# A dynamic convolution with two gated layers on one core: another order of the sequence, a buffer per tap product, a split by bank

## The chip, the cores and the metric

The kernel runs on one core of a Trainium2 chip. The core has a matrix engine (PE, TensorE), a vector engine (DVE, VectorE), a scalar engine (ACT, ScalarE), a fourth engine for elementwise work (POOL, GpSimd), an engine that only issues transfers (SP, SyncE), and 16 DMA engines that carry the transfers of all queues. The metric is the device time of one execution in microseconds; less is better.

## The reference, cut to what matters

```python
def _attn_ref(x, weight_gen):                      # x 2 x 4096 x 192, 8 heads, 7 taps
    w = np.exp(weight_gen - weight_gen.max(-1, keepdims=True))
    w = w / (w.sum(-1, keepdims=True) + 1e-09)
    x_pad = np.concatenate([np.zeros((B, 6, D)), x], axis=1)
    x_unf = x_pad[:, np.arange(S)[:, None] + np.arange(7)[None, :], :].reshape(B, S, 7, 8, 24)
    return np.einsum('bshk,bskhg->bshg', w, x_unf)
...
x = x.reshape(8192, 192)
x = (1 / (1 + np.exp(-(x @ w_gate)))) * (x @ w_val) @ w_out      # 192 -> 1536 -> 192
h = x @ w_in;  out = (h * np.cos(h)) @ w_out2                    # 192 -> 2048 -> 192
```

Each token is a softmax-weighted sum of itself and the six tokens before it, per head. Then come two layers. x is float32; the five weight matrices arrive as 64-bit floats, 8 bytes a number.

## The kernel before, in words

**Layout.** The 8192 tokens lie on 128 partitions of 64 tokens each. A chunk is 4 tokens of every partition (512 tokens), 16 chunks in all. The six tokens of padding before a partition's first token belong to the partition before it, so chunk 0 needs one load of its own four tokens and, for the padding, two more loads from the neighbouring partitions (`load_x`); chunk 1 loads eight tokens and copies two from chunk 0's buffer on POOL. Later chunks load ten tokens in one transfer.

**The convolution of a chunk.** After the softmax of the chunk's weights (`softmax_ops`, DVE and one Exp on ACT), DVE makes seven products, one for each tap (`tap`). For chunks 0 to 2, PE transposes each product and adds the seven up in PSUM (`transposes`, two banks, one for each half of the partitions). Chunk 0 is made by `first_input`: its products go through two buffers (`product_tile`), so the third product waits until PE has read the first. Between the products PE runs matmuls on the identity, one after each of the first six and four after the last (`warm_up`). Chunks 1 and 2 have a buffer for each product (`conv_products`).

**High and low parts.** Every float32 operand of the layers is split into a high part that PE multiplies exactly and a low part, the rest. The transposed input of chunks 0 and 1 is split by `split_input` with `fast` set: first six instructions on ACT for high parts (`L349`), then four on DVE (`L351`), then ten subtractions on DVE for the low parts (`L355`).

**The layers.** A step of layer 1 takes 128 columns of gate and value weights: 18 matmuls of 512 columns (`hidden`, `L407`; the last six need the low parts of the input), a sigmoid on ACT (`gate`, `L509`), the product on DVE (`L512`), high part on ACT (`L547`), low part on POOL (`L548`), and two or more steps later 10 output matmuls (`L426`). The banks of a step are free again after its product, and there are two pairs of banks, so step 2's matmuls wait for step 0's gate and product. Twelve steps make a chunk of layer 1. The segments run layer 1 of chunks 0 and 1, then layer 2 and layer 1 in turn.

**The weights.** They stay on the chip, as units: units 0 and 1 of layer 1 serve one step each, units 2 to 6 two steps each; three output units (o0, o1, o2) serve four steps each. A unit has a gate half and a value half (192 KB each for units 0 and 1, 384 KB each for the others); an output unit has 768 KB. x for a later chunk is 960 KB. A unit is decoded from 64-bit floats by two ACT instructions (`L109`, `L112`) and one on DVE (`L114`), then ACT makes its high part (`L119`) and POOL its low part (`L121`, for output units `L183`). `decoding` is a chain over all units in the order of their use; one `next` finishes a unit and starts the ACT part of the next one. `late` holds the high and low parts until they are run.

**The order** is that of the program on each engine; an engine takes its instructions one after another, and what is written first on ACT, DVE or POOL also runs first. Loads are issued on SP's queue, and at the start also on ACT's queue (`act`). The program has eight semaphores for transfers, used in turn, so an issue can wait for an earlier transfer to land, and the instructions behind it on its engine wait as well.

## Time and profile before

| | us |
|---|---|
| median of three runs (lowest, highest) | 1270.26 (1268.09, 1271.26) |
| profiled execution | 1270.46 |
| its span | 1268.6 |
| PE busy in the span | 1230.6 |
| DVE, ACT, POOL busy | 902.2, 795.2, 710.8 |

An engine is busy while an instruction of its own runs; the time in brackets ahead of an instruction is how long its engine stood idle before it, and behind the arrow stands what ended that. The granted clock of PE is given as a share of 2.4 GHz: 1.00 is 2.4 GHz, 0.50 is 1.2 GHz.

### The profile page before, as it was taken

To read this page: it belongs to the slowest core of one execution; us is meant where nothing else is said; L and a number is where in the kernel's file an instruction comes from. 1 tells how busy PE (TensorE), PEld (TensorE's weight loads), DVE (VectorE), ACT (ScalarE), POOL (GpSimd) and SP (SyncE) were. 2 spreads that over 40 slices of the span, in tenths; PEclk is the share of its full clock that TensorE was granted. 3 is DMA by queue.
4 is the path that set the end of the run, shared out by engine and by line. 5 is a ranking of instruction groups with operands and counts; after the bars stand their busy time and mean duration, and the time that the engine had idled before them with its cause. 6 is when DMAs were issued, how large, how long until landed. Compare 5 with 4: busy or idle time off the path is not lost.

```text
span 1268.6 us, 26949 instructions
## 1 busy us (share of the span) xinstructions
PE 1230.6 (97%) x11076; PEld 1051.6 (83%) x11076; DVE 902.2 (71%) x1307; ACT 795.2 (63%) x1328; POOL 710.8 (56%) x529
## 2 busy tenths in 40 slices
...
GB/s 211 200 110 26 58 37 81 26 45 32 33 58 26 74 32 45 26 38 57 27 59 48 43 28 26 69 27 49 51 21 50 26 71 26 13 51 14 1 26 25
DMA packets 26971, 62.33 MB, mean 49 GB/s; under 512 B 2530, under 2 KB 7010, under 8 KB 26848
## 3 DMA queue, kind: packets, MB, share of 16 engines
...
## 4 chain that ended last, share of the span: by engine, by line
PE 71%; DVE 7%; ACT 5%; issue 2%; POOL 0%; DVEq 0%; ACTq 0%
PE ph L407 39%; PE po L426 31%; DVE acc L302 2%; DVE wk L512 1%; ACT L533 1%; ACT wk L509 1%; ACT wk L533 1%; ACT gh L547 1%; DVE wk L537 1%; DVE wk L520 1%; DVE va L436 1%; ACT wk L527 1%; PE pt L328 1%; DVE wk L528 1%; DVE wk L523 0%
## 5 line engine op out<-in xcount | busy, mean ns | idle before, releaser
L548 POOL TENSOR_TENSOR gl<-wk,gh 128x512 fp32r<-128x512 f32 x446 | 606.5, 1366 | 506.3 <-ACT gh L547 389.3
L407 PE MATMUL ph<-xT,unit 64*128 64x512 f32 x5760 | 776.6, 391 | 15.1 <-ACT unit L119 3.7
L407 PEld LDWEIGHTS ph<-xT,unit 64*128 64x128 f32 x5760 | 615.6, 186 | 113.9 <-DVE wk L512 10.5
L426 PE MATMUL po<-gh,outu 64*128 64x512 f32 x2688 | 557.2, 390 | 4.7 <-ACT gh L547 1.8
L426 PE MATMUL po<-gl,outu 64*128 64x512 f32 x1792 | 469.4, 387 | 4.5 <-POOL gl L548 4.4
L426 PEld LDWEIGHTS po<-gh,outu 64*128 64x128 f32 x2688 | 407.8, 184 | 52.3 <-DVE va L436 9.2
L547 ACT ACTIVATE gh<-wk 128x512 fp32r<-128x512 f32 (+1 forms) x450 | 282.8, 628 | 254.0 <-DVE wk L512 190.7
L426 PEld LDWEIGHTS po<-gl,outu 64*128 64x128 f32 x1792 | 321.2, 184 | 32.0 <-POOL gl L548 6.1
L512 DVE TENSOR_TENSOR wk<-ph,wk 128x512 f32<-128x512 f32 x192 | 131.9, 687 | 153.5 <-ACT wk L509 127.3
L537 DVE SCALAR_TENSOR_TENSOR wk<-ph,wk 128x512 f32<-128x512 f32 (+1 forms) x258 | 167.0, 686 | 39.6 <-ACT wk L533 39.6
L533 ACT ACTIVATE wk<-wk,sin_bias 128x512 f32<-128x512 f32 (+1 forms) x258 | 171.2, 713 | 9.9 <-DVE wk L523 3.3
L509 ACT ACTIVATE wk<-ph 128x512 f32<-128x512 f32 x192 | 114.0, 594 | 63.7 <-PE ph L407 62.9
L520 DVE TENSOR_SCALAR wk<-ph 128x512 f32<-128x512 f32 x129 | 88.0, 683 | 71.3 <-PE ph L407 64.5
L527 ACT ACTIVATE wk<-ph 128x512 int32<-128x512 f32 x129 | 75.7, 587 | 78.5 <-PE ph L407 77.8
L276 DVE TENSOR_TENSOR pr<-xp,sm 128x768 f32<-128x768 f32 x89 | 101.0, 1137 | 2.2 <-PE pt L328 1.2
L302 DVE TENSOR_TENSOR acc<-acc,pr 128x768 f32<-128x768 f32 x78 | 100.9, 1294 | 0.4
L523 DVE SCALAR_TENSOR_TENSOR wk<-wk,ph 128x512 f32<-128x512 f32 x129 | 88.2, 684 | 4.4
L528 DVE TENSOR_TENSOR wk<-wk,ph 128x512 f32<-128x512 int32 x129 | 87.4, 678 | 0.0
L436 DVE TENSOR_TENSOR va<-po,va 128x512 f32<-128x512 f32 x32 | 22.0, 688 | 38.4 <-PE po L426 32.2
L355 DVE TENSOR_TENSOR xT<-pt,xT 64x256 fp32r<-64x256 f32 (+1 forms) x76 | 27.3, 414 | 21.5 <-ACT xT L349 21.3
L121 POOL TENSOR_TENSOR unit<-wf,unit 128x768 fp32r<-128x768 f32 (+1 forms) x11 | 22.9, 2080 | 31.6 <-ACT unit L119 31.6
L349 ACT ACTIVATE xT<-pt 64x256 fp32r<-64x256 f32 (+1 forms) x68 | 20.5, 377 | 23.4 <-PE pt L328 23.3
...
## 6 DMA issues: line engine op xcount, KB each, us to landing
...
rawo<-in_moe_w_out_dram SPq DMA_DIRECT2D x7, 768.0 KB, 20.2
...
```

The lines of the kernel that those rows point to most:

```text
L276: nc.vector.tensor_tensor(out=out.rearrange("p t (h g) -> p t h g", g=G), in0=xp[c][:, k:k + TC, :].rearrange("p t (h g) -> p t h g", g=G) ...
L302: nc.vector.tensor_tensor(out=acc, in0=acc, in1=last, op=ALU.add)
L407: nc.tensor.matmul(ps[i], lhsT=u.t[r, w, (s + i) % NQ, c0:c0 + P], rhs=xt[r, x, s, :], start=n == 0, stop=n == len(terms) - 1,)
L426: nc.tensor.matmul(po[2 * i + a], lhsT=w[r, d0:d0 + P], rhs=g[r], start=first and g is gh and d0 < D, stop=last and g is gl,)
L509: nc.scalar.activation(out=self.w[0], in_=self.ps[0], func=AF.Sigmoid)
L512: nc.vector.tensor_tensor(out=self.w[0], in0=self.ps[1], in1=self.w[0], op=ALU.mult)
L520: nc.vector.tensor_scalar(out=w, in0=u, scalar1=0.25, scalar2=ROUND_MAGIC, op0=ALU.add, op1=ALU.add)
L528: nc.vector.tensor_tensor(out=w, in0=w.bitcast(I32), in1=u, op=ALU.subtract)
L533: nc.scalar.activation(out=w, in_=w, func=AF.Sin, scale=-SIN_SCALE, bias=sin_bias)
L537: nc.vector.scalar_tensor_tensor(out=w, in0=self.ps[i][:, r], scalar=TWO_PI, in1=w, op0=ALU.mult, op1=ALU.mult)
L547: nc.scalar.activation(out=gh, in_=w, func=AF.Copy)
L548: eng.tensor_tensor(out=gl, in0=w, in1=gh.bitcast(F32), op=ALU.subtract)
```

## The change

It has four parts. (1) The chunks start at each partition's eighth tile and wrap round (`ROT` = 8), so chunk 0 has its padding in the same partition and comes in one transfer of ten tokens; chunk 1 loads four tokens and copies six from chunk 0's buffer; the chunks that need padding from the neighbouring partition are now the last two, 14 and 15. The weights of the softmax of chunk 0 and of chunks 1 and 2 come in two transfers in place of one. (2) `first_input` uses `conv_products`, with a buffer for each product, and the ten matmuls on the identity between them are gone. (3) The high parts of the split of chunks 0 and 1 go by bank: those of the first bank on ACT, those of the second on DVE, five instructions each. (4) The value halves of units 3 to 6 are issued on SP's queue and not on ACT's, and `first_input` takes three steps of `decoding` where it took two.

```diff
--- before.py
+++ after.py
@@ -59,6 +59,7 @@
     DA = P
     DC = D - DA
     NQ = D // HP
+    ROT = PAD + TC - PAD % TC
     LAG = 4
 
     xf = x.rearrange("b s d -> (b s) d")
@@ -211,13 +212,17 @@
     group_at = {t0 // TC: g for g, (t0, _) in enumerate(groups)}
     sm = {}
 
-    def load_group(g, tiles, tag, q=nc.sync):
-        t0, t1 = groups[g][0], groups[g + tiles - 1][1]
-        pool = opool if tag == "o" else fpool
+    def load_group(g, tag, q=nc.sync):
+        t0, t1 = groups[g]
+        pool = fpool if tag == "wf" else opool
         s = pool.tile([P, (t1 - t0) * H, K], F32, name="sm", tag=tag)
-        q.dma_start(
-            out=s.rearrange("p a k -> p (a k)"), in_=wgr[:, t0:t1, :].rearrange("p t c -> p (t c)")
-        )
+        cuts = sorted({t0, t1, min(max(t0, T - ROT), t1)})
+        for a, b in zip(cuts, cuts[1:]):
+            r = (a + ROT) % T
+            q.dma_start(
+                out=s[:, (a - t0) * H:(b - t0) * H, :].rearrange("p a k -> p (a k)"),
+                in_=wgr[:, r:r + b - a, :].rearrange("p t c -> p (t c)"),
+            )
         for t in range(t0, t1):
             sm[t] = (s, t0)
 
@@ -248,12 +253,14 @@
 
     xp = {}
 
-    def load_x(c, queues=(nc.sync, nc.sync)):
-        t0 = c * TC
+    def load_x(c):
+
+
+        t0 = (c * TC + ROT) % T
         pool, tag = (xpool, "xp") if c else (tpool, "xC")
         t = pool.tile([P, TC + PAD, D], F32, name="xp", tag=tag)
-        h = max(0, PAD - t0)
-        if c == 0:
+        h = PAD if c == 1 else max(0, PAD - t0)
+        if h and c != 1:
             for b in range(B):
                 nc.gpsimd.memset(t[b * per_batch:b * per_batch + 1, 0:h, :], 0.0)
         nc.sync.dma_start(out=t[:, h:, :], in_=xr[:, t0 - PAD + h:t0 + TC, :])
@@ -262,7 +269,7 @@
         elif h:
             for b in range(B):
                 p0 = b * per_batch
-                queues[b % 2].dma_start(
+                nc.sync.dma_start(
                     out=t[p0 + 1:p0 + per_batch, 0:h, :], in_=xr[p0:p0 + per_batch - 1, T - h:T, :]
                 )
         xp[c] = t
@@ -304,7 +311,7 @@
 
     def conv_products(c):
 
-        big = tpool.tile([P, K - 3, TC, D], F32, name="prs", tag="xA" if c % 2 == 0 else "xB")
+        big = tpool.tile([P, K - 3, TC, D], F32, name="prs", tag="xA" if c == LEAD else "xB")
         att[c] = [big[:, k] for k in range(K - 3)] + [product_tile(), product_tile(), acc_tile()]
         for k, pr in enumerate(att[c]):
             tap(c, k, pr)
@@ -343,8 +350,9 @@
             v = p[h][src, i * TC * HP:(i + 1) * TC * HP].rearrange("p (t n) -> p t n", n=HP)
             yield xt[dst, x, s].rearrange("p (t h n) -> p h t n", h=2, n=HP)[:, h], v
 
-    def high(eng, xt, p, slot):
-        for hi, v in columns(xt, 0, p, slot):
+    def high(xt, p, slot, engines):
+
+        for (hi, v), eng in zip(columns(xt, 0, p, slot), engines):
             if eng is nc.scalar:
                 eng.activation(out=hi, in_=v, func=AF.Copy)
             else:
@@ -371,13 +379,11 @@
     def split_input(xt, p, fast):
 
 
-        for slot in (OWN[0], OTHER[0], OWN[1]) if fast else OWN:
-            high(nc.scalar, xt, p, slot)
-        yield
-        if fast:
-            for slot in OTHER[1:]:
-                high(nc.vector, xt, p, slot)
-        for slot in (OWN[0], *OTHER[:2], OWN[1], OTHER[2]) if fast else OWN:
+        slots = (OWN[0], *OTHER[:2], OWN[1], OTHER[2]) if fast else OWN
+        for slot in slots:
+            high(xt, p, slot, (nc.scalar, nc.vector if fast else nc.scalar))
+        yield
+        for slot in slots:
             low(xt, p, slot)
         if not fast:
             exchange(xt)
@@ -385,15 +391,15 @@
     def first_input():
 
         p = [ps_o.tile([P, N], F32, name="pt", tag=f"po{2 * h}") for h in range(2)]
-        for k in range(K):
-            pr = product_tile()
-            tap(0, k, pr)
-            transposes(p, pr, k == 0, k == K - 1)
+        for k, _ in enumerate(conv_products(0)):
+            transposes(p, att[0][k], k == 0, k == K - 1)
             yield
         xt = xT[1, 0] = tpool.tile([P, 2, NQ, N], F32R, name="xT", tag="xA")
-        for _ in split_input(xt, p, True):
+        ops = split_input(xt, p, True)
+        next(ops)
+        yield
+        for _ in ops:
             pass
-        yield
 
     def hidden(u, c0, xt):
 
@@ -469,7 +475,7 @@
         nc.scalar.activation(out=o.rearrange("p t (x d) -> p t x d", d=HP)[:, :, 0::2, :], in_=p0, func=AF.Copy)
         nc.vector.tensor_copy(out=o[:, :, HP:DA], in_=p1[:, :, 0, :])
         nc.vector.tensor_tensor(out=o[:, :, DA:D], in0=p1[:, :, 1, :], in1=o[:, :, DA:D], op=ALU.add)
-        nc.sync.dma_start(out=outr[:, c * TC:(c + 1) * TC, :], in_=o)
+        nc.sync.dma_start(out=outr[:, (c * TC + ROT) % T:(c * TC + ROT) % T + TC, :], in_=o)
 
 
     xT = {}
@@ -631,8 +637,9 @@
     with tc.manual_schedule():
         nc.gpsimd.memset(sin_bias, SIN_BIAS)
         make_identity(nc, ident)
-        load_group(0, 2, "o", nc.scalar)
-        load_x(0, (nc.sync, nc.scalar))
+        load_group(0, "va", nc.scalar)
+        load_x(0)
+        load_group(1, "o", nc.scalar)
         sp, act = nc.sync, nc.scalar
         units1[0].load(sp, 0)
         units1[0].load(act, 1)
@@ -689,27 +696,27 @@
         for ops in [s0] * 3 + [s1] * 2 + [s0] * 2 + [s1] * 3:
             next(ops)
         nc.scalar.activation(out=warm, in_=sin_bias, func=AF.Sigmoid)
+        units1[3].load(sp, 1)
         load_x(1)
         units1[4].load(sp, 0)
+        units1[4].load(sp, 1)
         outs1[1].load(sp)
-        units1[5].load(sp, 0)
         for _ in s0:
             pass
         warm_up(NWARM)
         for k, _ in enumerate(first_input()):
-            if k in (3, 5):
+            if k in (5, 6):
+                next(decoding)
+            if k == 5:
+                run(late)
+            if k == K:
+                run(late)
                 next(decoding)
                 run(late)
-            if k == 2:
-                units1[3].load(act, 1)
-                units1[4].load(act, 1)
-            if k == K:
-                units1[5].load(act, 1)
-                units1[6].load(sp, 0)
-                units1[6].load(act, 1)
-                outs1[2].load(sp)
-            else:
-                warm_up(1 if k < K - 1 else 4)
+        for i in 5, 6:
+            units1[i].load(sp, 0)
+            units1[i].load(sp, 1)
+        outs1[2].load(sp)
         for st in steps[:2]:
             st.mm_high()
 
@@ -795,9 +802,9 @@
             if layer == 1 and j == st.nj - 2 and c + 2 < NCH:
                 load_x(c + 2)
                 if c + 4 in group_at and group_at[c + 4] > 2:
-                    load_group(group_at[c + 4], 1, "wf")
+                    load_group(group_at[c + 4], "wf")
             if layer == 2 and c == 0 and j == 5:
-                load_group(2, 1, "wf")
+                load_group(2, "wf")
         for q in waiting:
             q.mm_out()
         steps[-1].finish()
```

**What the change moves, on ACT.** Before, from the decoding of unit 2 (`wf<-raw 128x768`) to the first gate (`wk<-ph`) and the high part of unit 2 (`unit<-wf 128x768`); the two rows `DMA raw<-in_moe_w_val_dram` issue the value halves of units 5 and 6, `wf<-rawo` decodes o0, and a name like DMAHW4 is one of the eight semaphores of transfers:

```order
L109 ACTIVATE wf<-raw 128x768 [waits DMAHW1_49]
L112 ACTIVATE raw<-raw 128x768
L119 ACTIVATE unit<-wf 128x384 [waits DVE_49]
L349 ACTIVATE xT<-pt 128x4x64 [waits PE_49] x2
L349 ACTIVATE xT<-pt 64x4x64 x4
L136 DMA raw<-in_moe_w_val_dram 64x3x512 [waits DMAHW4_49]
L136 DMA raw<-in_moe_w_val_dram 64x3x512 [waits DMAHW6_49]
L109 ACTIVATE wf<-rawo 128x768 [waits DMAHW2_49,Pool_49]
L112 ACTIVATE rawo<-rawo 128x768
L509 ACTIVATE wk<-ph 128x512 [waits PE_49]
L119 ACTIVATE unit<-wf 128x768 [waits DVE_49,Activation_49]
```

The same place now, up to the high part of o0 (`outu<-wf`); the first `wf<-raw 128x768` is unit 2, the second, after o0, is unit 3:

```order
L110 ACTIVATE wf<-raw 128x768 [waits DMAHW7_49,DMAHW0_49]
L113 ACTIVATE raw<-raw 128x768
L357 ACTIVATE xT<-pt 128x4x64 [waits PE_49]
L357 ACTIVATE xT<-pt 64x4x64 x4
L120 ACTIVATE unit<-wf 128x384 [waits DVE_49]
L110 ACTIVATE wf<-rawo 128x768 [waits DMAHW1_49,Pool_49]
L113 ACTIVATE rawo<-rawo 128x768
L120 ACTIVATE unit<-wf 128x768 [waits DVE_49]
L110 ACTIVATE wf<-raw 128x768 [waits DMAHW3_49,DMAHW2_49,Pool_49]
L113 ACTIVATE raw<-raw 128x768
L515 ACTIVATE wk<-ph 128x512 [waits PE_49]
L120 ACTIVATE outu<-wf 128x4x192 [waits DVE_49]
```

The issues are gone from between the split of chunk 0 (`xT<-pt`) and the decoding of o0; the decoding of unit 3 now stands ahead of the first gate, and waits for two transfers.

**On DVE.** Before, the seven taps of chunk 0 (`pr<-xp,sm`), the decoding of units 0 and 1 between them, the four high parts (`CAST`) and the first low parts (`xT<-pt,xT`):

```order
L276 TENSOR_TENSOR pr<-xp,sm 128x768 [waits DMAHW2_49,DMAHW3_49,DVE_49,Pool_49]
L276 TENSOR_TENSOR pr<-xp,sm 128x768
L276 TENSOR_TENSOR pr<-xp,sm 128x768 [waits DVE_49,PE_49]
L276 TENSOR_TENSOR pr<-xp,sm 128x768 [waits DMAHW1_49,DVE_49,PE_49]
L114 SCALAR_TENSOR_TENSOR wf<-wf,raw 128x384 [waits DMAHW5_49,DMAHW4_49,Activation_49]
L276 TENSOR_TENSOR pr<-xp,sm 128x768 [waits DVE_49,PE_49] x2
L114 SCALAR_TENSOR_TENSOR wf<-wf,raw 128x384 [waits DMAHW6_49,DMAHW0_49,Activation_49]
L276 TENSOR_TENSOR pr<-xp,sm 128x768 [waits DVE_49,PE_49]
L351 CAST xT<-pt 64x4x64 [waits PE_49,Activation_49] x2
L351 CAST xT<-pt 64x4x64 x2
L355 TENSOR_TENSOR xT<-pt,xT 128x4x64 x2
L355 TENSOR_TENSOR xT<-pt,xT 64x4x64 x2
```

The same place now, the seven taps into `prs`, `pr` and `acc`:

```order
L283 TENSOR_TENSOR prs<-xp,sm 128x768 [waits DMAHW1_49,DVE_49]
L283 TENSOR_TENSOR prs<-xp,sm 128x768 x3
L283 TENSOR_TENSOR pr<-xp,sm 128x768 x2
L115 SCALAR_TENSOR_TENSOR wf<-wf,raw 128x384 [waits DMAHW4_49,DMAHW3_49,Activation_49]
L283 TENSOR_TENSOR acc<-xp,sm 128x768
L115 SCALAR_TENSOR_TENSOR wf<-wf,raw 128x384 [waits DMAHW6_49,DMAHW5_49,Activation_49]
L359 CAST xT<-pt 128x4x64 [waits PE_49]
L359 CAST xT<-pt 64x4x64 x4
L115 SCALAR_TENSOR_TENSOR wf<-wf,raw 128x768 [waits DMAHW7_49,DMAHW0_49,Activation_49]
L363 TENSOR_TENSOR xT<-pt,xT 128x4x64 [waits Activation_49]
```

The taps no longer wait for PE, the high parts wait for PE alone and not for ACT, and the decoding of unit 2 stands between the high and the low parts.

**On SP.** Before, the first issues (`xp` is x, `rawo` an output unit):

```order
L259 DMA xp<-in_x_dram 128x768
L265 DMA xp<-in_x_dram 63x1152
L136 DMA raw<-in_moe_w_gate_dram 64x3x256 x2
L136 DMA raw<-in_moe_w_gate_dram 64x3x512
L168 DMA rawo<-in_moe_w_out_dram 128x4x384
L136 DMA raw<-in_moe_w_gate_dram 64x3x512
L259 DMA xp<-in_x_dram 128x1536
L136 DMA raw<-in_moe_w_gate_dram 64x3x512
L168 DMA rawo<-in_moe_w_out_dram 128x4x384
```

And now:

```order
L266 DMA xp<-in_x_dram 128x1920
L137 DMA raw<-in_moe_w_gate_dram 64x3x256 x2
L137 DMA raw<-in_moe_w_gate_dram 64x3x512
L169 DMA rawo<-in_moe_w_out_dram 128x4x384
L137 DMA raw<-in_moe_w_gate_dram 64x3x512
L137 DMA raw<-in_moe_w_val_dram 64x3x512
L266 DMA xp<-in_x_dram 128x768
L137 DMA raw<-in_moe_w_gate_dram 64x3x512
L137 DMA raw<-in_moe_w_val_dram 64x3x512
L169 DMA rawo<-in_moe_w_out_dram 128x4x384
```

The two loads of x at the start became one of ten tokens, and each gate half from unit 3 on is followed by its value half; x of chunk 1 is half as wide and stands behind unit 3's value half.

## Rows read from the trace of the kernel before

**Rows 1.** Busy time of each engine (and instructions) by stretches of 80 us.
```profile
80.00:160.00 80.00, 70.36 (x630) 58.21 (x629) 56.84 (x67) 55.12 (x88) 53.99 (x37) 0.94 0.12 33
160.00:240.00 80.00, 79.69 (x714) 67.00 (x712) 63.56 (x95) 51.59 (x87) 47.29 (x35) 1.00 0.17 47
```
**Rows 2.** The same by stretches of 10 us: clock, DMA share and GB/s last.
```profile
0.00:10.00 10.00, 3.78 (x16) 3.48 (x16) 3.13 (x10) 3.08 (x5) 2.79 (x9) 1.00 0.83 193
10.00:20.00 10.00, 8.57 (x90) 7.03 (x90) 6.95 (x8) 4.75 (x9) 2.07 (x2) 1.00 1.11 189
20.00:30.00 10.00, 9.14 (x73) 6.72 (x72) 6.33 (x15) 2.47 (x7) 1.32 (x2) 1.00 1.06 255
30.00:40.00 10.00, 5.13 (x24) 3.14 (x25) 5.45 (x10) 7.46 (x11) 4.57 (x3) 0.72 1.10 184
```
**Rows 3.** Timeline of PE: start us, us, instructions, idle time before and its releaser.
```profile
22.10 1.11 PE L328 MATMUL pt<-ident,pr 64*128 64x64 f32 x16
...
35.41 1.65 PE L407 MATMUL ph<-xT,unit 64*128 64x512 f32 x6 [3.68 <-ACT unit L119]
...
42.89 2.22 PE L407 MATMUL ph<-xT,unit 64*128 64x512 f32 x18
...
61.81 5.21 PE L407 MATMUL ph<-xT,unit 64*128 64x512 f32 x30 [2.06 <-POOL unit L121]
...
72.12 2.04 PE L328 MATMUL pt<-ident,prs 64*128 64x64 f32 x62 [0.52 <-DVE wk L512]
...
82.64 2.65 PE L407 MATMUL ph<-xT,unit 64*128 64x512 f32 x18 [1.44 <-DVE xT L355]
```
**Rows 4.** Timeline of ACT; ACTq rows are issues of transfers.
```profile
16.06 0.55 ACT L109 ACTIVATE wf<-raw 128x384 f32<-128x384 f32 x1 [5.19 <-DMA raw<-in_moe_w_gate_dram]
...
23.25 2.00 ACT L349 ACTIVATE xT<-pt 128x256 fp32r<-128x256 f32 x6 [2.04 <-PE pt L328]
29.84 2.54 ACTq L136 DMA_DIRECT2D raw<-in_moe_w_val_dram  x2
32.49 0.89 ACT L109 ACTIVATE wf<-rawo 128x768 f32<-128x768 f32 x1 [7.24 <-DMA raw<-in_moe_w_gate_dram]
...
34.04 0.58 ACT L509 ACTIVATE wk<-ph 128x512 f32<-128x512 f32 x1
34.52 0.84 ACT L119 ACTIVATE unit<-wf 128x768 fp32r<-128x768 f32 x1
```
**Rows 5.** Timeline of DVE.
```profile
8.68 0.39 DVE L246 TENSOR_TENSOR sm<-sm,st 128x224 f32<-128x224 f32 x1
10.12 2.11 DVE L276 TENSOR_TENSOR pr<-xp,sm 128x768 f32<-128x768 f32 x2 [1.06 <-DMA xp<-in_x_dram]
...
17.08 0.56 DVE L114 SCALAR_TENSOR_TENSOR wf<-wf,raw 128x384 uint32<-128x384 uint32 x1 [1.77 <-ACT raw L112]
...
25.01 1.55 DVE L351 CAST xT<-pt 64x256 fp32r<-64x256 f32 x4 [3.49 <-ACT xT L349]
26.59 3.89 DVE L355 TENSOR_TENSOR xT<-pt,xT 128x256 fp32r<-128x256 f32 x10
...
111.03 7.03 DVE L276 TENSOR_TENSOR prs<-xp,sm 128x768 f32<-128x768 f32 x1
```
**Rows 6.** The transfer issued at 11.96 us: KB, us to landing.
```profile
xp<-in_x_dram SPq DMA_DIRECT2D x1, 768.0 KB, 17.9
```
**Rows 7.** The transfer issued at 15.88 us.
```profile
rawo<-in_moe_w_out_dram SPq DMA_DIRECT2D x1, 768.0 KB, 21.3
```
**Rows 8.** Timeline of POOL.
```profile
1.29 2.15 POOL L258 MEMSET xp<- 1x1152 f32 x2
10.05 0.50 POOL L261 COPY xp<-xp 128x384 f32<-128x384 f32 x1 [6.61 <-DMA xp<-in_x_dram]
...
37.87 1.29 POOL L548 TENSOR_TENSOR gl<-wk,gh 128x512 fp32r<-128x512 f32 x1
39.12 2.69 POOL L183 TENSOR_TENSOR outu<-wf,outu 128x256 fp32r<-128x256 f32 x2
```
## The prediction, made before the changed kernel was run

> **What bounds the kernel now.** I read the busy time by long stretches first. From 160 us on PE is busy 79.69 of 80 us at the full granted clock [rows 1]; its instructions are the same after the change, but for ten matmuls on the identity, so nothing can be won or lost there unless a new wait arises. Between 80 and 160 us PE is idle for 9.6 us, and the clock is granted at 0.94. The rest of what can move lies in the first 80 us. There the stretches of 10 us show the DMA engines busy throughout, at 193, 189, 255 and 184 GB/s [rows 2]: 1.93 MB have come by 10 us, 3.82 MB by 20, 6.37 MB by 30, 8.21 MB by 40. PE is busy only 5.13 us of the ten from 30 to 40 us, at a mean clock of 0.72.
>
> PE's timeline tells why [rows 3]. The transposes of chunk 0 end at 23.2 us (22.10 + 1.11). Step 2 starts at 35.41 us, after 3.68 us of idle time, and step 3 only at 42.89. At 61.81 us PE has waited 2.06 us for POOL's low part of a unit, and at 82.64 us 1.44 us for the low parts of chunk 1's input. On ACT [rows 4] the cause of 35.41 stands: the high parts of the input end at 25.25, and then ACT runs nothing until 32.49, an idle time of 7.24 us, because two issues of value halves stand in its queue and wait until 29.84 us and later for transfers to land. Behind them stand the decoding of o0, the first gate (34.04) and the high part of unit 2 (34.52). DVE's timeline [rows 5] shows the earlier part: the softmax ends at 9.07, the first tap starts at 10.12 when x has landed, and four high parts wait 3.49 us for ACT's.
>
> **The change, step by step.** All times are of the profiled execution (1270.46 us, a span of 1268.6 and 1.9 around it), which lies 0.2 us over the median of the runs.
>
> *Taps.* The weights of chunk 0's softmax (112 KB in place of 336) run beside one x transfer of 960 KB on the other queue; both were there by 10.12 before, with the same bytes. The first tap can start between 8.0 (my estimate for a softmax that ends 1 us before the 9.07 of now) and 10.1 (as now). I take 9.4, since the weights are fewer but share with a larger x. Seven taps without waits for PE cost at most 1.05 us each (two took 2.11 beside POOL's copy [rows 5]; the copy grows from 0.50 us to some 1.5 [rows 8], so I keep this price for all): 7.4. The decoding of unit 0 between them costs 0.56, the last 16 transposes 1.11. The transposes end at 18.5, 4.7 us earlier than 23.2. Transposes of 1.11 us a tap keep up with taps of 1.05 but for a few tenths.
>
> *High and low parts.* ACT made six in 2.00 us, DVE four in 1.55 [rows 4, 5]: five each, side by side, end at 20.5. On DVE the decoding of unit 2 now stands ahead of the low parts, twice the columns of one that took 0.56, so about 1.0; the low parts take 3.89 as before. They end at 25.4, against 30.48: 5.1 us earlier. The first high part on ACT also stands behind the decoding of unit 2; it costs nothing if that unit lands by 17, and up to 3 us if by 20.
>
> *The gate of step 0.* Here the change adds a wait. ACT is now free of issues, but ahead of the gate stand the decoding of o0 and of unit 3 (a pair of instructions takes 1.55 us, from 32.49 to 34.04) and the high part of unit 2; and behind the gate stands everything on ACT, so DVE's product and PE's step 2 wait too. When do the units land? Up to o0 the new order issues x 0.98 MB, softmax weights 0.34, units 0 and 1 0.79, unit 2 0.79 and o0 0.79: 3.69 MB, which by the rates of [rows 2] have come at 19.3; with unit 3 4.48 MB, at 22.6. A transfer lands later than its bytes in order: x of chunk 1, 5.27 MB with all issued before it, would be there at 25.7, and landed at 11.96 + 17.9 = 29.9 [rows 6], 4.2 us late; the output unit issued at 15.88, at 6.85 MB, would be there at 32.6 and landed at 37.2 [rows 7], 4.6 late. The lag is bounded by 0 and 4.6; I take 4.2. So o0 lands at 23.5, unit 3 at 26.8. ACT: o0 from 23.5 to 25.05, unit 2's high part to 25.9, a wait to 26.8, unit 3 to 28.35, then the gate. The first two steps' low terms are done by about 27 and are covered. From gate to step 2 it is 1.37 us (34.04 to 35.41): step 2 at 29.7, 5.7 us earlier; with a lag of 0, bound by the low parts, 8 us.
>
> *Step 3* comes after the output matmuls of step 0, and these need o0's low part and step 0's low part on POOL. o0's high part follows the gate on ACT, to 29.7; POOL then takes 2.69 for o0 and 1.29 for the step [rows 8], to 33.7; ten matmuls take about 1 us. Step 3 at 34.7, against 42.89: 8.2 us earlier. This is more than at step 2, because before, step 2 ran at the lower clock: six matmuls in 1.65 us, 0.275 each, where 18 take 2.22, 0.123 each [rows 3].
>
> *To the end of chunk 0.* The decoding of o1 stands ahead of step 2's gate. Its bytes, 6.45 MB, are there at 30.4, with the lag at 34.9; the gate comes at 36.5, then unit 4's high part, its low part on POOL and step 2's low part behind that, so the output matmuls of step 2 wait. This takes back 1.4 us: 6.8 remain. Later units arrive ahead of their use. One more step of decoding is done ahead of step 0, so each unit's low part stands one place further up in POOL's queue than before; the wait of 2.06 us at 61.81 should go, and with it the slow matmuls behind it (30 in 5.21 us, where 0.123 each give 3.7): 3.6 us. If POOL is as late as before, nothing. I take 3.6: 10.4.
>
> *Chunk 1.* The two-sided split takes 1.9 + 3.9 us where it took 7.2, so the wait of 1.44 us at 82.64 goes: 11.8. The other losses up to 160 us I leave as they are; they come from collisions of POOL and DVE, such as one tap of 7.03 us [rows 5], that no order shows, and I bound this by 4 us either way.
>
> *What costs nothing.* Chunks 14 and 15 get two memsets on POOL each (2.15 us for the larger pair [rows 8]) and two more transfers each; POOL is busy for only 47.29 of 80 us once the layers run evenly [rows 1] and x is loaded a whole layer-2 segment ahead. Without that cover it would be 2 to 4 us. SP's four more issues wait in place of ACT's; behind them stands x of chunk 1, which landed at 29.9 before, and whose products PE transposes at 72.1 [rows 3]. The load of x for chunk 1 is smaller by 0.39 MB, which is in the sums.
>
> Sum: 4.7 at the transposes becomes 5.7 at step 2, 8.2 at step 3, 6.8 at step 5, 10.4 at the end of chunk 0 and 11.8 after the split of chunk 1. 1270.46 - 11.8 = 1258.7, against the median 1258.5.
>
> **The clock.** The first transposes run at 69 ns each (16 in 1.11 us), those of chunk 1 at 33 (62 in 2.04) [rows 3], so PE was at the pace of the lower clock then, although the column of the granted clock reads 1.00 in those rows [rows 2]. Ten matmuls on the identity leave this stretch, and PE waits for the high parts without them. The Trainium skill, "TensorE: Matmul & The Clock Gate", section on the HAM clock gate, says that the throttled clock is the default, that only sustained activity releases it and that idle time takes it back; by it steps 0 to 2 would run at 1.2 GHz, and the time would be that of the first rival below, not the sum above. No row here shows the start without those matmuls.
>
> **Rivals.**
> - *Lower clock to step 3.* Step 2 (18 matmuls) and the ten output matmuls behind it take 0.15 us more each, 4.3, of which POOL's low parts cover 1.6; step 3 adds 2.7 before the clock is back. It gives back 2.7 to 5.4: 1261 to 1264. For it: the idle time at the start. Against it: steps 0 and 1 give PE 36 matmuls between 19 and 27 us.
> - *Weights set the pace.* The lag grows by 3 us, since all halves now go through one queue, and POOL's wait at unit 5 comes back because its work is as dense as before. 6.8 - 3 + 1.4 = 5: 1265. For it: the DMA engines are busy throughout.
> - *More is won.* Chunk 1 is relieved by the step of decoding that was done ahead; 4 us of its losses go: 1254.
> - *The gain is lost again.* POOL and DVE collide once more with a tap like the one of 7.03 us and a slow clock behind it, 5 + 3.4 us, in chunk 0 or 1: 1267, no change.
> - *Slower.* The gate of step 0 stands behind unit 3. If unit 3 landed after 32.5 (32.5 + 1.55 = 34.04), the gate would be later than now; at 38 us it costs 5.5, and 1276 is the time. Against it: by 38 us the rates bring 7.8 MB, and unit 3 needs 4.48.
>
> **Chances.** The forecast (1255 to 1262) 0.45, weights 0.20, clock 0.12, more 0.08, lost again or nothing done 0.10, slower 0.05. A difference of 0.3% (3.8 us) is about what a measurement of this kernel tells from none. Faster 0.85, same 0.10, slower 0.05. The range goes from 1252 (the forecast with the lag at 1 us and part of chunk 1's losses gone) to 1266 (weights at their worst); the cases outside hold about 0.18.
>
> **What would show it.** Right: the last transpose of chunk 0 ends near 18.5; no idle time of 7 us on ACT; step 2 near 29.7 and step 3 near 34.7; no waits of 2 us for a unit's low part near 50 us; the transposes of chunk 1 some 10 us earlier than 72.1. Wrong: ACT waiting for unit 3 or o1 past 30 and 38 us, PE at half clock through step 3, or a wait in chunks 14 and 15.

## The result

The changed kernel took 1255.09 us (median of 4 runs, 1254.03 to 1256.62), the kernel before 1269.17 beside it (1268.06 to 1271.26): a ratio of 0.9876, 95% interval 0.9858 to 0.9894. The forecast was 1258.5, its range 1252 to 1266. The profiled execution of after took 1254.05 us with a span of 1252.3, which is 16.3 us less than the span of before. One of the four executions of run 1 below took 1355.79 us at a mean clock of 0.85, a slow state that is not the kernel's, and is left out of that run's median.

Busy time by stretches of 10 us, and then of 80 us, of the changed kernel. The columns, here and in [rows 1, 2], are the stretch and its length, the busy time of PE, of PE's loading of weights, of DVE, ACT and POOL (with the number of instructions), the granted clock, the DMA share and GB/s:

```profile
0.00:10.00 10.00, 3.79 (x16) 3.49 (x16) 3.52 (x11) 2.30 (x4) 1.89 (x8) 0.95 0.85 248
10.00:20.00 10.00, 7.54 (x119) 6.62 (x121) 9.50 (x15) 7.67 (x16) 1.57 (x1) 0.67 1.08 261
20.00:30.00 10.00, 8.35 (x54) 5.83 (x52) 8.25 (x18) 9.31 (x14) 6.71 (x5) 0.87 1.07 237
30.00:40.00 10.00, 8.98 (x74) 6.82 (x76) 9.09 (x9) 7.72 (x12) 9.98 (x7) 1.00 1.08 238
40.00:50.00 10.00, 8.97 (x79) 6.86 (x77) 10.00 (x10) 8.00 (x12) 10.00 (x6) 1.00 1.08 234
50.00:60.00 10.00, 7.99 (x66) 5.85 (x62) 10.00 (x8) 7.60 (x11) 10.00 (x6) 1.00 1.08 267
...
80.00:160.00 80.00, 73.61 (x688) 61.12 (x686) 60.89 (x76) 57.78 (x93) 60.24 (x44) 0.98 0.18 47
160.00:240.00 80.00, 79.71 (x714) 66.84 (x712) 61.16 (x90) 49.59 (x84) 45.56 (x33) 1.00 0.15 43
```

From 160 us on nothing changed, as forecast. PE's 5.13 busy us from 30 to 40 became 8.98. What the forecast did not have stands in two columns: the DMA engines move 248 and 261 GB/s in the first 20 us, where [rows 2] have 193 and 189, and POOL is busy for 30 us on end from 30 us on, DVE for nearly as much.

PE's timeline of after, with the places of [rows 3]:

```profile
10.89 3.73 PE L335 MATMUL pt<-ident,prs 64*128 64x64 f32 x64 [5.70 <-DVE prs L283]
14.40 1.75 PE L335 MATMUL pt<-ident,pr 64*128 64x64 f32 x32
16.57 0.69 PE L335 MATMUL pt<-ident,acc 64*128 64x64 f32 x16 [0.41 <-DVE acc L283]
...
26.27 2.33 PE L413 MATMUL ph<-xT,unit 64*128 64x512 f32 x17 [0.70 <-DVE wk L518]
...
31.01 2.20 PE L413 MATMUL ph<-xT,unit 64*128 64x512 f32 x18
...
48.70 4.41 PE L413 MATMUL ph<-xT,unit 64*128 64x512 f32 x35 [1.02 <-DVE wk L518]
...
60.49 2.04 PE L335 MATMUL pt<-ident,prs 64*128 64x64 f32 x62 [0.78 <-DVE wk L518]
...
69.94 2.65 PE L413 MATMUL ph<-xT,unit 64*128 64x512 f32 x18 [0.39 <-DVE xT L363]
...
118.05 2.11 PE L335 MATMUL pt<-ident,prs 64*64 64x64 f32 x61
```

Set against [rows 3], this is the lead at each place: 5.9 us at the last transpose of chunk 0 (17.26 for 23.2), 9.1 at step 2 (26.27 for 35.41), 11.9 at step 3, 11.6 at the transposes of chunk 1, 12.7 behind the split of chunk 1, and 16.4 at the transposes of chunk 2, for which the row of the kernel before is

```profile
134.47 2.13 PE L328 MATMUL pt<-ident,prs 64*128 64x64 f32 x62
```

No wait for a unit's low part is left near 50 us; short waits for DVE's products stand in its place.

ACT's timeline of after, where [rows 4] have 7.24 us of idle time and the gate at 34.04:

```profile
17.70 1.96 ACT L357 ACTIVATE xT<-pt 128x256 fp32r<-128x256 f32 x5
19.68 0.52 ACT L120 ACTIVATE unit<-wf 128x384 fp32r<-128x384 f32 x1
20.11 0.93 ACT L110 ACTIVATE wf<-rawo 128x768 f32<-128x768 f32 x1
...
22.45 0.91 ACT L110 ACTIVATE wf<-raw 128x768 f32<-128x768 f32 x1
...
24.14 0.60 ACT L515 ACTIVATE wk<-ph 128x512 f32<-128x512 f32 x1
...
30.25 0.90 ACT L110 ACTIVATE wf<-rawo 128x768 f32<-128x768 f32 x1
```

No row here has an idle time: o0 (20.11), unit 3 (22.45) and o1 (30.25) had all landed when ACT came to them, the last piece of each at 15.85, 19.25 and 29.48 us. ACT works without a pause from the split to the gate.

### The profile page after: what moved, and what is told of

Read it like the earlier page. It is cut to its first block, busy times and chain, and to the rows that moved or that the text cites. A ratio compares the mean times of both kernels' runs of the same rounds, so it can differ in the third digit from the quotient of the medians.

```text
span 1252.3 us, 26914 instructions
## 1 busy us (share of the span) xinstructions
PE 1218.8 (97%) x11056; PEld 1024.8 (82%) x11056; DVE 901.0 (72%) x1309; ACT 794.2 (63%) x1326; POOL 712.7 (57%) x531
## 4 chain that ended last, share of the span: by engine, by line
PE 76%; DVE 6%; ACT 3%; issue 1%; POOL 0%; DVEq 0%; ACTq 0%
PE ph L413 42%; PE po L432 33%; DVE acc L309 2%; DVE wk L518 1%; ACT wk L515 1%; DVE wk L526 1%; ACT gh L553 1%; DVE va L442 1%; PE pt L335 1%; DVE wk L534 1%; DVE wk L543 0%; ACT wk L539 0%; ACT L539 0%; DVE wk L529 0%; ACT wk L533 0%
## 5 line engine op out<-in xcount | busy, mean ns | idle before, releaser
L413 PEld LDWEIGHTS ph<-xT,unit 64*128 64x128 f32 x5760 | 605.5, 185 | 116.3 <-DVE wk L518 13.6
L283 DVE TENSOR_TENSOR pr<-xp,sm 128x768 f32<-128x768 f32 x84 | 96.0, 1143 | 0.0
```

What stands on the lines that cost most here:

```text
L283: nc.vector.tensor_tensor(out=out.rearrange("p t (h g) -> p t h g", g=G), in0=xp[c][:, k:k + TC, :].rearrange("p t (h g) -> p t h g", g=G) ...
L413: nc.tensor.matmul(ps[i], lhsT=u.t[r, w, (s + i) % NQ, c0:c0 + P], rhs=xt[r, x, s, :], start=n == 0, stop=n == len(terms) - 1,)
```

## Experiments

The theories: **A**, the steps of the prediction (ACT's issues waited for transfers, the taps for buffers, POOL for its turn, and each part of the change removes one). **B**, two issuing queues slow the transfers. **C**, the queue matters little. **D**, the loads over 63 partitions, which the kernel before makes for the padding, slow the transfers behind them. All but one of the kernels are the changed kernel with one thing put back, added or moved; "step 2", "step 3" and "chunk 1" below are the starts on PE of these steps and of the transposes of chunk 1 (26.27, 31.01, 60.49 in after, 35.41, 42.89, 72.12 in before). A step counts from its second matmul, because in some kernels the first runs ahead alone, in after at 25.19.

| kernel | median us | ratio to before, 95% | step 2 | chunk 1 |
|---|---|---|---|---|
| after | 1255.09 | 0.9876 (0.9858, 0.9894) | 26.27 | 60.49 |
| 1 value halves on ACT | 1255.30 | 0.9872 (0.9855, 0.9889) | 26.35 | 60.56 |
| 2 before, new load order alone | 1266.35 | 0.9962 (0.9949, 0.9976) | 31.72 | 68.35 |
| 3 no rotation | 1258.15 | 0.9894 (0.9879, 0.9910) | 28.84 | 64.35 |
| 4 old split | 1257.95 | 0.9893 (0.9878, 0.9907) | 27.54 | 61.75 |
| 5 two product buffers | 1256.12 | 0.9888 (0.9869, 0.9907) | 27.41 | 61.64 |
| 6 identity matmuls back | 1259.80 | 0.9919 (0.9904, 0.9935) | 31.27 | 65.50 |
| 7 two decode steps | 1258.83 | 0.9909 (0.9890, 0.9928) | 25.48 | 63.73 |
| 8 spare loads, 63 x 768 B | 1254.37 | 0.9871 (0.9849, 0.9892) | 26.44 | 60.66 |
| 9 spare loads, 64 x 768 B | 1255.32 | 0.9880 (0.9860, 0.9899) | 26.70 | 60.93 |
| 10 spare loads, 63 x 4608 B | 1262.62 | 0.9939 (0.9924, 0.9954) | 30.64 | 67.24 |
| 11 spare loads, 64 x 4608 B | 1257.79 | 0.9904 (0.9887, 0.9920) | 27.92 | 64.13 |
| 12 first decode at the fourth tap | 1256.00 | 0.9887 (0.9868, 0.9905) | 27.12 | 61.34 |

**1. The value halves of units 3 to 6 on ACT's queue again.**

```diff
-        units1[3].load(sp, 1)
+        units1[3].load(act, 1)
```

(and the same for units 4, 5 and 6)

> The changed kernel, with the value halves of units 3 to 6 issued on ACT's queue again, at the same places of the program. Theory A (ACT was held by the issues' waits; on its own queue each issue waits for a transfer eight places earlier): ACT is held again behind the high parts of chunk 0, where it now goes from 19.7 us straight on; the transfers it would wait for land at 17 to 21 us now, so it is held 1 to 4 us, and the kernel takes 1256 to 1260 us. Theory B (with two queues the DMA engines themselves are slower: 193 and 189 GB/s in the first two stretches of 10 us before, 248 and 261 now): the stretch from 10 to 20 us falls under 220 GB/s, everything that waits for weights is 4 us or more late, 1260 to 1264 us.

The time did not change beyond the measurement, so the times of A and B both missed, and from 10 to 20 us there is no fall of the rate as B has it. The mechanism of A does show, at the low end: ACT's two issues stood at 20.24 and 22.68, and the second waited for unit 4's value half, which landed at 22.66. Behind it stood the decoding of unit 3, whose own halves had landed by 17.95; it started at 23.38, after 1.15 us of idle time, and the gate came 0.8 us later. Step 2 did not move, because DVE, which decodes o0 ahead of the product, came to it at 25.60, in after at 25.54. In the changed kernel the queue costs nothing in the time; this does not show what it cost before.

**2. The kernel before, with only the order and queue of the loads as in the change.**

```diff
+        units1[3].load(sp, 1)
         load_x(1)
         units1[4].load(sp, 0)
+        units1[4].load(sp, 1)
         outs1[1].load(sp)
-        units1[5].load(sp, 0)
...
-            if k == 2:
-                units1[3].load(act, 1)
-                units1[4].load(act, 1)
```

(and all halves of units 5 and 6, then o2, on SP behind the first input)

> The kernel before, with only the queue and the order of the weight loads of the changed one (value halves of units 3 to 6 on SP). Theory A: the 7.24 us in which ACT stood idle go; the first gate follows the low parts (30.5 us) at some 31.5 in place of 34.0, and without the long idle time PE keeps its clock, so step 3 starts 4 to 6 us earlier: 1263 to 1266 us. Theory B: the same, and the DMA rate from 10 to 20 us rises from 189 to over 230 GB/s. Theory C (the queue matters little, the early start of the taps and the decoding step carry the gain): 1267 to 1270 us.

By the ratio 4.8 us of the gain come from this alone, as A has it; step 3, at 39.15, was 3.7 us earlier. ACT's timeline shows the idle time of [rows 4] gone and another one in its place:

```profile
22.51 2.00 ACT L349 ACTIVATE xT<-pt 128x256 fp32r<-128x256 f32 x6 [2.80 <-PE pt L328]
24.40 0.88 ACT L109 ACTIVATE wf<-rawo 128x768 f32<-128x768 f32 x1
...
29.55 0.60 ACT L509 ACTIVATE wk<-ph 128x512 f32<-128x512 f32 x1 [3.48 <-PE ph L407]
```

o0 is decoded at 24.40 instead of 32.49, and the gate then waits for PE. The transposes still end at 22.5, and the wait of 2.06 us for POOL is still there (at 58.04). B falls too: with one queue for the halves of units 3 to 6 the DMA engines moved 206, 181, 196 and 192 GB/s in the first four stretches of 10 us, no more than before.

**3. No rotation: the first chunk is again the sequence's own, with its padding from two loads over 63 partitions (on SP and on ACT).**

```diff
-    ROT = PAD + TC - PAD % TC
+    ROT = 0
...
-                nc.sync.dma_start(
+                (nc.scalar if b and c == 0 else nc.sync).dma_start(
```

> The changed kernel without the rotation: chunk 0 has its padding in the neighbouring partitions again, three loads of x on two queues in place of one. Theory A (the prediction's: the same bytes, no other rate): the first tap starts when x lands, at about 10.1 us in place of 9.9, and the kernel takes 1255 to 1256.5 us. Theory D (the narrow loads over 63 partitions hold up the loads behind them; the rates of 248 and 261 GB/s come from the one wide transfer): from 0 to 20 us the rate falls to about 200 GB/s, the weights come 3 to 5 us later, 1258 to 1260 us.

2.3 us slower by the ratios, in the time that D gave. The second group of the softmax weights, behind the padding on ACT's queue, held DVE for 3.90 us, and the first tap came at 12.13 instead of 9.87. That start, 2.3 us later, is most of the 2.6 us at step 2. The rates fell to 212, 224, 191 and 201 GB/s, although all loads but those of chunk 0 were the same. This is why D was tested in runs 8 to 11.

**4. The split as before: ACT's high parts first, DVE's after them.**

```diff
-        for slot in slots:
-            high(xt, p, slot, (nc.scalar, nc.vector if fast else nc.scalar))
+        for slot in (OWN[0], OTHER[0], OWN[1]) if fast else OWN:
+            high(xt, p, slot, (nc.scalar, nc.scalar))
         yield
+        if fast:
+            for slot in OTHER[1:]:
+                high(xt, p, slot, (nc.vector, nc.vector))
```

> The changed kernel with the high parts of chunks 0 and 1 as before: six on ACT, then four on DVE. Theory A: the low parts end 1.3 us later in both chunks; in chunk 0 the first gate then waits for PE and moves by about as much, in chunk 1 the wait of 0.39 us before the first low term grows to 1.4 us or more: 1256.5 to 1258 us. Rival (hidden by the decoding of unit 2 that DVE now does between high and low parts, and by POOL, which is busy without a pause from 30 to 64 us): 1255 us, no change.

2.2 us slower by the ratios, as A has it. Step 2 came 1.3 us later, and at 73.78 the wait of PE for the low parts of chunk 1 was back at 1.43 us; [rows 3] have 1.44.

**5. Two product buffers for chunk 0, without the identity matmuls.**

```diff
-        for k, _ in enumerate(conv_products(0)):
-            transposes(p, att[0][k], k == 0, k == K - 1)
+        for k in range(K):
+            pr = product_tile()
+            tap(0, k, pr)
+            transposes(p, pr, k == 0, k == K - 1)
```

> The changed kernel with the old pair of product buffers for chunk 0: tap k waits again until the transposes of product k-2 are done (tap k of before waited 1.06 us there), everything else as changed. Theory A (the taps' waits on PE were part of what held the transposes): the last transpose ends 2 to 4 us after 17.3 us, step 2 starts near 29, and all of it is kept until chunk 1: 1257 to 1259 us, ratio to the kernel before 0.990. Rival (with the ten identity matmuls gone the transposes are done before the next tap needs its buffer, so the buffers no longer bound anything): last transpose by 17.8 us, ratio within 0.002 of the changed kernel's 0.988.

Nearer to the rival: the last transpose ended at 18.02, 0.76 us later, step 2 1.1 later, and the time rose by 1.0 to 1.5 us, no more than the measurement can tell. DVE waited only twice for PE, 0.35 us each. (The 1.06 us in the expectation were the wait for x in [rows 5]; the taps of before waited 0.35 and 0.81 us for PE.)

**6. The ten identity matmuls back.**

```diff
                 next(decoding)
                 run(late)
+            else:
+                warm_up(1 if k < K - 1 else 4)
```

> The changed kernel with the ten identity matmuls back between chunk 0's transposes (one after each of products 0 to 5, four after product 5's, as in the kernel before). Theory A (TensorE's clock in these 10 us is no term: it was at 0.67 from 10 to 20 us in the changed kernel and at 1.00 with a value load on ScalarE's queue, and step 2 came at 26.27 and 26.35): step 2 within 0.4 us of 26.3 us, 1254.5 to 1256.5 us. Rival (the identity matmuls held the half-speed clock off, and leaving them out cost the chain from the last transpose to step 2): step 2 at 25.0 to 25.7 us, 1253 to 1254.5 us.

Both expectations were wrong: 5.5 us slower by the ratios, the costliest of the parts put back. PE's timeline shows why (L630: each identity matmul shows as two instructions):

```profile
10.53 1.11 PE L335 MATMUL pt<-ident,prs 64*128 64x64 f32 x16 [5.34 <-DVE prs L283]
11.57 0.79 PE L630 MATMUL pw<-ident 128*128 128x128 f32 x2
12.30 1.12 PE L335 MATMUL pt<-ident,prs 64*128 64x64 f32 x16
...
21.14 1.11 PE L335 MATMUL pt<-ident,acc 64*128 64x64 f32 x16
22.18 2.07 PE L630 MATMUL pw<-ident 128*128 128x128 f32 x8
```

From 10.53 on PE has no pause: each product costs it 1.77 us (10.53 to 12.30), and the seventh is through at 22.25, although DVE had made the last tap by 16.15 and every product has a buffer. The 5.0 us by which this is later than in after stand unchanged at step 2 (31.27 for 26.27) and at the transposes of chunk 1 (65.50 for 60.49). In the kernel before the same rows stand 1.77 us apart too, from 11.43 to the 22.10 of [rows 3], six intervals of 1.78:

```profile
11.43 1.11 PE L328 MATMUL pt<-ident,pr 64*128 64x64 f32 x16 [6.24 <-DVE pr L276]
12.47 0.79 PE L624 MATMUL pw<-ident 128*128 128x128 f32 x2
13.19 1.11 PE L328 MATMUL pt<-ident,pr 64*128 64x64 f32 x16
```

PE was its own bound there, and the taps waited for buffers only because PE was late.

The clock that was granted, of this kernel, in stretches of 4 us (12 to 16, 16 to 20, 20 to 24):

```profile
12.00:16.00 4.00, 4.00 (x41) 3.09 (x41) 4.00 (x6) 1.77 (x5) 0.07 (x1) 0.50 1.08 290
16.00:20.00 4.00, 4.00 (x48) 3.32 (x50) 0.62 (x2) 1.47 (x2) 1.49 (x1) 0.50 1.07 258
20.00:24.00 4.00, 4.00 (x36) 3.50 (x32) 1.59 (x4) 1.63 (x5) 0.00 (x0) 0.50 1.07 239
```

and of the changed kernel:

```profile
12.00:16.00 4.00, 4.00 (x80) 4.00 (x76) 4.00 (x6) 1.79 (x5) 0.00 (x0) 0.53 1.08 286
16.00:20.00 4.00, 2.43 (x29) 1.51 (x27) 3.50 (x8) 3.89 (x9) 1.57 (x1) 0.90 1.08 258
20.00:24.00 4.00, 4.00 (x25) 3.17 (x23) 3.89 (x11) 4.00 (x6) 2.48 (x2) 0.67 1.05 217
```

PE was busy throughout with the identity matmuls and had half the clock for all of it; without them it was at 0.90 from 16 to 20 us. (The clock of 1.00 that the expectation has for run 1 from 10 to 20 us is no measurement: the first clock record of that trace is at 16.27.)

**7. Two decode steps in the first input's stretch instead of three.**

```diff
                 run(late)
-                next(decoding)
-                run(late)
```

> The changed kernel with two decode steps of the weights in the first input's stretch, as before, instead of three; the third is left to the steps of chunk 0. Theory A (the step done ahead relieves the decode work of chunks 0 and 1, where POOL and DVE run without a pause from 30 to 64 us): steps 2 and 3 start as in the changed kernel or some tenths earlier (26.3 and 31.0 us), but one decode more is left in a stretch that is full, the waits of PE for POOL grow, and the transposes of chunk 1 start 2 to 4 us after 60.5 us: 1257 to 1259 us. Rival (the place of a decode step is free, since ACT and DVE have room elsewhere): 1254.5 to 1256 us, and the transposes of chunk 1 within 0.7 us of 60.5.

4.2 us slower by the ratios, as A has it (3.7 by the medians). Step 2 got going earlier, at 25.48 without a pause behind its first matmul, but stood still after six matmuls for unit 2's low part, 1.55 us; step 3 came at 33.13, and further on PE shows the row that [rows 3] have at 61.81:

```profile
50.40 0.96 PE L413 MATMUL ph<-xT,unit 64*128 64x512 f32 x6
53.42 5.16 PE L413 MATMUL ph<-xT,unit 64*128 64x512 f32 x30 [2.06 <-POOL unit L122]
```

The wait is the same to the hundredth, and so, nearly, is the pace of the 30 matmuls behind it (5.21 us before).

**8 and 9. Two spare loads of one row (768 bytes) on each of 63, or of 64, partitions, behind chunk 0's load.** Nobody reads them.

```diff
         load_x(0)
+        for b in range(B):
+            p0 = b * per_batch
+            nc.sync.dma_start(out=spare[p0 + 1:p0 + per_batch, :], in_=xr[p0 + 1:p0 + per_batch, 0, :])
```

(`p0` instead of `p0 + 1` for 64)

> The changed kernel with two transfers added right behind chunk 0's: 63 partitions with one row of 768 bytes each, twice, into a tile that nobody reads (97 KB in all, some 0.4 us at 240 GB/s). All three kernels seen so far with chunk 0's pads loaded over 63 partitions (before, before with the new order of loads, the changed kernel without the rotation) moved 181 to 224 GB/s from 10 to 20 us and 1536-byte packets took 113 to 163 ns there; the three with one transfer of 128 partitions moved 254 to 295 GB/s at 84 to 86 ns. Theory D (a transfer over 63 partitions upsets how the later ones run): 10 to 20 us at 180 to 225 GB/s, 1536-byte packets over 110 ns up to 60 us, step 2 starts 1 to 3 us after 26.3 us, 1256 to 1259 us. Rival (the pads' own bytes or their place in the memory cost, not the count of partitions): rates of 10 to 60 us stay at 234 to 267 GB/s, packets near 86 ns, time 1255 to 1256 us.

> The same two spare transfers as in the run beside it, each over 64 partitions instead of 63 (1.5 KB more in all). Theory D (63 partitions upset the later transfers, 64 don't): rates of 10 to 60 us as in the changed kernel, 234 to 267 GB/s, 1536-byte packets under 100 ns from 10 to 30 us, time 1255 to 1256 us. Rival (any further transfer of short rows at that place does it, whatever its count of partitions): rates and packets as in the run with 63 partitions.

D failed in this form: both kernels took the time of the changed one, with step 2 within 0.4 us. With 63 partitions the rates from 10 to 30 us were somewhat lower (231 and 224 GB/s, 252 and 249 with 64), and the packets as quick.

**10 and 11. The same with six rows (4608 bytes) a partition, as the padding of before has them.** Spare loads of 581 and 590 KB into a tile that is free until the split.

```diff
         load_x(0)
+        spare = tpool.tile([P, 2 * NQ, N], F32, name="spare", tag="xA")
+        for b in range(B):
+            p0 = b * per_batch + 1
+            p1 = (b + 1) * per_batch
+            nc.sync.dma_start(
+                out=spare[p0:p1].rearrange("p a n -> p (a n)")[:, 0:PAD * D],
+                in_=xr[p0:p1, 0:PAD, :].rearrange("p t d -> p (t d)"),
+            )
```

(`b * per_batch` for 64)

> The changed kernel with a copy of the old pads' transfers that nobody needs: twice 63 partitions with six rows (4608 bytes) each, behind chunk 0's transfer, into a tile that is free until the split of chunk 0's input; 581 KB in all. The two spare transfers of one row each left the packets of 1536 bytes at 88 to 102 ns up to 40 us. Theory D2 (transfers like the pads' set the later ones back, not only by their bytes): 1536-byte packets over 110 ns from 10 to 40 us and under 225 GB/s in the windows of 10 to 50 us, as in the three kernels with pads. Rival (bytes alone): the loads behind land some 2.4 us later (581 KB at 240 GB/s), rates of 10 to 50 us stay at 234 GB/s or more and packets under 105 ns. Theory A for the time: the value half of unit 3, read without a wait at 22.4 us in the changed kernel, is late by up to 3 us, ScalarE waits for it, step 2 at 26.3 to 29 us, 1255 to 1258 us.

> The same spare transfers as in the run beside it, each over 64 partitions (590 KB). If the count of 63 partitions is what sets the later transfers back, rates and packets here are as in the changed kernel (237 to 261 GB/s from 10 to 40 us, 1536-byte packets under 105 ns) while the run beside it is slow; if any such transfer does it, both are slow alike; if bytes alone count, neither is. Time by theory A as in the run beside it, or up to 1.5 us shorter if only 63 partitions do harm.

Here 63 and 64 part: 1262.62 and 1257.79 us, the smaller load being the slower one by 4.8 (4.4 by the ratios, with some 3 us of uncertainty; the profiled spans are 2.9 apart). Rates and packets are as D2 has them; the time and step 2, at 30.64, lie beyond the ranges given for run 10. Stretches of 10 us from 10 to 40 us, first with 63, then with 64 partitions:

```profile
10.00:20.00 10.00, 5.03 (x96) 4.89 (x96) 8.95 (x17) 4.84 (x9) 0.19 (x1) 0.57 1.04 201
20.00:30.00 10.00, 7.57 (x53) 5.54 (x53) 9.09 (x21) 8.58 (x15) 4.23 (x3) 0.83 1.08 205
30.00:40.00 10.00, 7.68 (x50) 4.80 (x50) 5.65 (x8) 6.97 (x11) 7.24 (x5) 1.00 1.09 195
```

```profile
10.00:20.00 10.00, 6.16 (x114) 5.63 (x114) 9.53 (x17) 7.05 (x13) 1.57 (x1) 0.67 1.10 234
20.00:30.00 10.00, 9.77 (x55) 7.70 (x54) 8.66 (x18) 7.62 (x12) 4.90 (x4) 0.69 1.07 241
30.00:40.00 10.00, 7.88 (x59) 5.19 (x57) 6.13 (x8) 8.08 (x12) 7.91 (x6) 1.00 1.09 220
```

The DMA share is the same, 1.04 to 1.10, and the bytes are not. The mean time of one packet of 1536 bytes (rows of the output units) between 10 and 40 us, worked out from the trace's records of packets, parts all kernels with such loads over 63 partitions from all without:

```
long loads over 63 partitions:  before 148 ns, run 2 157, run 3 135, run 10 147
none:  after 92 ns, run 11 96, all other runs 86 to 97
```

And the forecast's wait for landings appears. ACT's timeline in run 10, where the three idle times are for the value halves of units 3 and 4 and for o1:

```profile
27.68 0.90 ACT L110 ACTIVATE wf<-raw 128x768 f32<-128x768 f32 x1 [1.09 <-DMA raw<-in_moe_w_val_dram]
...
33.65 0.90 ACT L110 ACTIVATE wf<-raw 128x768 f32<-128x768 f32 x1 [2.40 <-DMA raw<-in_moe_w_val_dram]
...
37.78 0.90 ACT L110 ACTIVATE wf<-rawo 128x768 f32<-128x768 f32 x1 [0.58 <-DMA rawo<-in_moe_w_out_dram]
```

Run 11 has waits for DMA at the same places (0.78, 2.01 and 0.57 us), so part of the loss is that of bytes. Its first tap starts at 10.91, that of run 10 at 13.40.

The traces also show how the load is shared. For each transfer a trace has the moments at which pieces of it were reported as landed, 16 for nearly every one. Each of the two spare transfers has 16 such moments in run 11 (7.29 to 8.22 and 9.10 to 10.10 us), but nine in run 10 (7.99 to 9.84 and 11.76 to 13.09), besides one each at 1.69 and 2.07, before the first of their packets (4.85); those of before and of runs 2, 3 and 8 over 63 partitions have nine as well. In run 10 no more than nine of their packets are under way at a time, in run 11 up to 16. And what follows lands in two groups in run 10: of the transfer issued at 7.65 us seven moments lie between 12.44 and 13.94 and nine between 16.68 and 17.77, of o1 seven by 35.57 and nine from 36.70 on; in run 11 the eighth follows the seventh within 0.4 us for every transfer issued in the first 50 us. That is how it looks when nine of the 16 DMA engines carry the narrow loads and stay behind the other seven; a transfer is there only with its last share.

The Trainium skill, "DMA: Bandwidth & Descriptors", section "Why a DMA increments its semaphore by 16 and not by 1", gives a rule for this: a transfer is shared among the largest number of DMA engines, at most 16, that divides the slowest dimension at both of its ends, and it takes the lowest-numbered ones; by it 64 partitions go to all 16, 63 to nine. The nine and the 16 moments of the traces agree with it; which engines they are no record here names. An estimate from that page and run 10's rows: 581 KB on nine engines are 64.5 KB each, at 4608 bytes in 345 ns 4.8 us; 590 KB on sixteen are 36.9 KB each, at run 11's 298 ns 2.4 us. The difference of 2.4 us is close to the 2.5 us between the first taps, and with 768 bytes a partition it would be some 0.3 us, which is not seen. Why a single packet takes longer behind the narrow loads, until 60 us and beyond, is not in it, and no run here tells.

**12. Unit 0's decode step two taps earlier, and unit 1's copies ahead of the split.**

```diff
-            if k in (5, 6):
-                next(decoding)
-            if k == 5:
-                run(late)
+            if k in (3, 6):
+                next(decoding)
+                run(late)
             if k == K:
-                run(late)
```

> The changed kernel with the decode step of unit 0 behind the fourth tap instead of the sixth, and unit 1's high and low parts ahead of the split of chunk 0's input. In the changed kernel ScalarE stands 2.21 us at 15.7 us for that step on VectorE. Theory A (ScalarE's row of work from the last transpose to the gate of step 0 sets step 2): it loses one copy of 0.5 us behind the transposes, step 2 0.3 to 0.5 us earlier, transposes end at most 0.1 us later, POOL starts its low parts 1.5 us earlier; 1253.5 to 1255 us. Rival (PE's matmuls of steps 0 and 1 end just as late, or the copy ahead delays the split): step 2 within 0.2 us of 26.3 or later, 1255 to 1256.5 us.

The rival's time and step 2 came: 1256.0 us and 27.12. Unit 1's copy waited 1.77 us for DVE and started at 17.77, the split on ACT at 18.20 instead of 17.70, and the gate waited 1.20 us for PE. But the 0.85 us at step 2 were lost before: POOL made unit 0's low part from 14.49 to 15.58, beside the fifth and sixth taps, and these two took 2.63 us (1.82 in after), so the last transpose ended at 18.11 instead of 17.26. What ACT's row alone is worth, this run does not show. No run beat the changed kernel by more than the measurement can tell.

## Why the prediction came out right, and where it was off

The parts put back one at a time (runs 3 to 7) cost, as differences of the ratios times 1270 us, 2.3, 2.2, 1.5, 5.5 and 4.2 us: 15.7 in all, against the 15.7 us of the ratio 0.9876. Each has some 3 us of uncertainty, and the queue of the value halves is not among them: it is worth nothing in the changed kernel (run 1), and with the order of the loads 4.8 us on the base of before (run 2). So the parts overlap, and the close agreement is chance.

The forecast is nearer at the end than its steps. Behind the split of chunk 1 it has 11.8 us where 12.7 were measured, but at step 3 it has 8.2 for 11.9, and from there to the transposes of chunk 1 it adds 2.2 where 0.3 were lost. That these errors cancelled is luck.

*Taps and transposes.* 4.7 us forecast, 5.9 measured, with the wrong cause. The prediction said that "seven taps without waits for PE" set the end of the transposes, as if the buffers had held them. Run 5 puts the buffers at 0.8 us of it; run 6, with all the buffers, ends the transposes at 22.25. It was the identity matmuls in PE's row, 0.7 us for each product at half the clock, that held them. The prediction gave no price to leaving them out, except a loss in its rival on the clock. The taps themselves started later than forecast (9.87 for 9.4) and took less (0.89 us each for 1.05).

*High and low parts.* Forecast to end at 25.4, measured 24.32; DVE's five high parts took 2.23 us, the low parts 3.87. Run 4 confirms this edit and the 1.44 us of chunk 1.

*The gate of step 0.* This term was mis-sized. The prediction took the rates of [rows 2] and "a lag of 4.2 us", so unit 3 would land at 26.8 and o1 at 34.9. They landed at 19.25 and 29.48, ACT decoded them at 22.45 and 30.25 without waiting, and step 2 came 3.4 us earlier than forecast (26.27 for 29.7), step 3 3.7 earlier (31.01 for 34.7). The prediction's other bound, "with a lag of 0, bound by the low parts, 8 us", was the nearer one: 9.1 us, with low parts that ended 1.1 us sooner than it had them. The rates were not the memory's or the engines' own: they were those of a kernel with two loads over 63 partitions ahead. So was the lag: of the transfer of [rows 6] seven moments lie between 24.76 and 26.09 us, about the 25.7 that the prediction worked out from the bytes, and the other nine between 28.97 and 29.82. With such loads in the changed kernel (run 10) step 2 came at 30.64 and step 3 at 36.58, beyond the forecast. The prediction counted the loads of the padding by their bytes alone.

*ACT's issues.* Right: run 2 moves step 2 by 3.7 us and the time by 4.8 with this alone. Run 1 shows that the queue of the value halves does not matter once the transfers land early.

*To the end of chunk 0.* The lead shrank by 1.4 us from step 3 to step 5, as forecast (11.9 at step 3; step 5 at 38.74, 49.24 before: 10.5), but that is luck, for o1's landing, the cause given, cost nothing; PE waited for POOL's low parts, 0.33 and 0.47 us, with ACT, DVE and POOL all full. Then 3.6 us were to come from POOL's wait. The wait went, and run 7 brings it back with 2.06 us there and 4.2 us in the time, so its cause, the decode step done ahead, holds. In the timeline, though, only 1.1 us showed (10.5 to 11.6), because waits of 1.02, 0.89, 0.82 and 0.78 us for DVE and ACT came up. POOL had idle gaps of 0.5 to 1.5 us in chunk 0 before and has none from 26.3 to 64 us now: the stretch has become POOL's and DVE's, and the 3.4 us won early were mostly lost to that.

*Chunk 1.* "The other losses up to 160 us I leave as they are" is the other step that was off, by 3.7 us, just inside the 4 us that the prediction allowed for it. From the transposes of chunk 1 to those of chunk 2 it took 62.35 us before and 57.56 after, and 1.1 of that is the split. In the kernel before, the tap of 7.03 us [rows 5] made DVE's product late; PE waited 2.00 us for it at 118.72 and then ran 18 matmuls in 4.31:

```profile
118.72 3.44 PE L407 MATMUL ph<-xT,unit 64*128 64x512 f32 x17 [2.00 <-DVE wk L512]
...
123.03 4.31 PE L407 MATMUL ph<-xT,unit 64*128 64x512 f32 x18 [0.86 <-ACT wk L509]
```

In after a tap of 6.14 us stands at 89.04 and once it is done PE waits 0.74 us at most at a time. The granted clock was at 0.50 for 10.2 us of this stretch before (from 106.0 and from 119.7 us), for 3.4 in after (from 90.9). The rival "more is won" put this down to the decode step done ahead. Run 7 speaks against that: without the step the stretch took 58.71. It took 57.5 to 60.1 in all the variants of the changed kernel and 61.07 in run 2, the only one on the base of before. In the eight variants at 59.0 or more the clock was at 0.50 for 3.4 us from within the transposes of chunk 1 on (run 1 from 60.64 us); in after and runs 10 and 11, at 57.5 to 57.6, it was not. So 1.5 of the 3.7 us hang on a fall of the clock that this one execution was spared. Which of the remaining edits moved the collision stays open.

*The clock.* The rival of the lower clock fell. By the rule that the prediction cites from the Trainium skill's "TensorE: Matmul & The Clock Gate", steps 0 to 2 would run slowly without the identity matmuls. The granted clock was at 0.67 and 0.87 from 10 to 30 us, so steps 0 and 1 ran at the lower level (1.2 GHz) in part, from 19.19 to 22.60 us, but it had risen before step 2, which ran 17 matmuls in 2.33 us, as at the full clock. Before had no clock record ahead of 24 us, and its column of 1.00 there says nothing: its transposes took 1.11 us for 16, as in run 6 at 0.50. The prediction read that pace rightly, but did not see that at this pace the identity matmuls held up the transposes.

*Chunks 14 and 15.* No wait appeared there: PE's idle time from 160 us to the end is 7.1 us in both kernels, and the lead of 16.4 us at chunk 2 is that of the whole span, 16.3.
